# Three split passes instead of full-width products in the 128-row groups of a second MoE (one core)

## The chip, the core and the metric

The kernel runs on one core of a Trainium2 chip. The metric is device time in microseconds, from one launch of the whole chain (attention, first MoE, second MoE). The engines are named as the profile names them: PE (TensorE's matmuls; PEld its weight loads), DVE (VectorE), ACT (ScalarE), POOL (GpSimd) and SP (SyncE, which issues most DMAs).

## What is computed

The reference, cut to the part that the change touches (before it come a windowed attention and a dense MLP with softplus, whose output is `x` here):

```python
def _moe2_ref(x, w_gate, w_noise, noise, w1, w2):      # x 2304 x 512, 8 experts
    ...                                                # noisy logits, top2 and weights top2_w
    for e in range(E):
        for k in range(2):
            mask = top2[:, k] == e
            h = np.maximum(x[mask] @ w1[e], 0.0)       # w1[e] 512 x 1024
            out[mask] += top2_w[mask, k, None] * (h @ w2[e])   # w2[e] 1024 x 512
    return out
```

All of it is float32.

## The kernel before, in words

The kernel writes its own order of instructions: a small planner (`Order`) keeps a clock of its own with a cost for each step, and emits ACT, DVE, POOL and SP work from a heap as PE's matmuls are written out. An engine then runs its instructions in that order. Attention and the first MoE end about 690 us into the run; the rest, what is looked at here, is the second MoE.

**Groups.** The routed rows of each expert are cut into groups of 256 rows ("pairs", `n == 2`) and of 128 rows ("singles", `n == 1`). The list `groups` holds 4 early pairs, 14 later pairs and 5 singles that always run, in the order 4 + 2 pairs, single, 3 pairs, single, 3 pairs, single, 6 pairs, single, single. Two further singles stand behind a condition and do not run with this input. A group gathers its rows from DRAM by an indirect DMA on POOL (`xg`), transposes them on PE (`g_transpose`), multiplies by `w1` (step `s1`, "up"), and by `w2` (step `s3`, "down"), and adds the weighted result to the output by an indirect DMA on POOL. A pair has 8 up and 8 down steps of 128 hidden columns; a single has 2 up and 2 down steps of 512, with a transpose of the relu output between them (`s2`), since it computes rows by hidden columns and not hidden columns by rows.

**The order on PE.** `phase2(x)` issues `s1` of step x, then a transpose for the next group if one is due, then `s2` of step x-1; the loop then issues `s3` of step x-2. The steps of all groups stand in one list, so around a single S the order is: up step 7 of the pair before, down 5; S up 0, transpose for the next group, down 6; S up 1, transpose for the next group, transpose of S's relu output 0, down 7; up 0 of the next group, transpose of S's relu output 1, S down 0; up 1 of the next group, S down 1.

**Precision.** A pair does its float32 products as three passes: each operand is cut into a high part (float32r, made by ACT) and a low part (the rest, made by DVE), and high x high, high x low and low x high are added up in PSUM (`up`, line 524, and `down`, line 536). A single takes its raw float32 weights and its float32 input in one plain product.

**Weights.** A group needs 8 pieces of 128 x 1024, 512 KB each: 4 of `w1` (kind 0) and 4 of `w2` (kind 1). `WJ` lists all pieces in one order, for a pair w1, w2, w1, w2, ..., for a single its 4 of w1 and then its 4 of w2 (line 1076). `w2_load` (line 1088) loads them in this order into 4 extra buffers and into a ring of 24 buffers. `w2_split` (line 1128) takes the next loaded piece, makes `whi` on ACT and `wlo` on DVE in two ring buffers, and gives the raw buffer back (`w2_drop`). At most `NSPLIT = 5` pieces are split and not yet used up. `w2_free` (line 1159) is called when PE has used a piece for the last time: it counts `nsplit` down for a split piece (for a raw one it gives the raw buffer back) and calls `pump`, which loads and splits what now has room. `skip_singles` moves the splitting past the pieces of singles.

The lines of the count, before the change:

```python
        if j >= wl[0] or not splitting[0] or nsplit[0] >= NSPLIT or nback[0] < len(sidx) or ring_left() < 2:
            return False
        wsp[0] += 1
        nsplit[0] += 1
        ...
        chain(("A", ca(1024), lambda: ACT.activation(hi, t, AF.Copy), None, (("r2", j),)),
              ("V", cv(1024), low, ("w2", j)))
```

Of the kernel before, what the change touches and what calls it, by code (L numbers as in the profile page):

```python
# [18 lines left out]
P = 128  # L19
# [6 lines left out]
class Order:  # L26
# [11 lines left out]
    def chain(self, *steps, after=0.0):  # L38

        heapq.heappush(self.heap, (self.now + after, self.count, steps, 0))  # L40
        self.count += 1
# [54 lines left out]
def ca(n):  # L96
    return 0.16 + n * 0.00083


def cv(n):  # L100
    return 0.15 + n * 0.00104
# [11 lines left out]
def moe_chain_kernel(ctx, tc, qk, v, w_in, w_out, w_gate, w_noise, noise, w1, w2, out):  # L113
# [939 lines left out]
    def g_transpose(g, a):  # L1053
        n, eo, i = groups[g]
        d = GR[g]
        pt = ps_t(("gx", g, a)).rearrange("p (c t) -> p c t", c=KC)
        for kc in range(KC):
            tr(pt[:, kc, :], d["xg"][a][:, kc * P:(kc + 1) * P], ident)
        if n == 1:
            d["xT"] = tl(p2, [P, KC, P], F32, "xs", 2, ("gup", g))  # L1060
            return chain(("A", ca(512), lambda: ACT.activation(d["xT"], pt, AF.Copy), ("gx", g, a)))
        if a == 0:
            d["xT"] = tuple(tl(mid, [P, KC, CT], F32R, x, 2, ("gup", g)) for x in ("xh", "xl"))
        xh, xl = d["xT"]
        sl = slice(a * P, (a + 1) * P)
        chain(("A", ca(512), lambda: ACT.activation(xh[:, :, sl], pt, AF.Copy)),
              ("V", cv(512), lambda: DVE.tensor_sub(xl[:, :, sl], pt, f32(xh[:, :, sl])), ("gx", g, a)))
# [20 lines left out]
    def w2_load():  # L1088
        j = wl[0]
        if j >= NW:  # L1090
            return False
        g, kind, f = WJ[j]
        if g >= sure[0] or ("tab", 2 if groups[g][0] == 1 else int(g >= NEARLY)) not in o_.fin:
            return False
        more = len(extra) < NXTRA
        if not more and (nback[0] < len(sidx) or ring_left() < 1 + 2 * max(1, NSPLIT - nsplit[0])):
            return False
        wl[0] += 1
        n, eo, i = groups[g]
        if g not in REG:  # L1100
            REG[g] = SP.value_load(TB[eo][0:1, 0, i:i + 1], min_val=0, max_val=E - 1)
            g_rows(g)
            if g < 3 or g - 3 in turned:
                g_start(g)
        if more:
            extra.add(j)
            t = p2.tile([P, 1024], F32, name="raw2", tag="raw2", bufs=NXTRA)
        else:
            inring[0] += 1
            t = wpool.tile([P, 1024], F32, name="rawp", tag="w", bufs=NRING)  # L1110
        RAW2[j] = t
        SP.dma_start(t, (w2 if kind else w1)[bass.ds(REG[g], 1), f].rearrange("e p n -> p (e n)"))
        chain(("SP", 0.5, None), ("DMA", (1 << 19) / 280e3, None), (None, 2.5, None, ("r2" if n == 2 else "w2", j)))
        if n == 1 and wsp[0] == j:
            skip_singles()
        return True

    turned = set()
# [2 lines left out]
        n = groups[g][0]  # L1121
        chain(("P", 1.3 * n, lambda: g_gather(g), ("gg", g), (("rows", g),)), (None, 3.0, None, ("gl", g)))

    def skip_singles():
        while wsp[0] < wl[0] and groups[WJ[wsp[0]][0]][0] == 1:
            wsp[0] += 1

    def w2_split():
        skip_singles()
        j = wsp[0]  # L1130
        if j >= wl[0] or not splitting[0] or nsplit[0] >= NSPLIT or nback[0] < len(sidx) or ring_left() < 2:
            return False
        wsp[0] += 1
        nsplit[0] += 1
        t = RAW2[j]
        hi, lo = W2[j] = [wpool.tile([P, 1024], F32R, name=x, tag="w", bufs=NRING) for x in ("whi", "wlo")]

        def low():
            DVE.tensor_sub(lo, t, f32(hi))  # L1139
            w2_drop(j)  # L1140
        chain(("A", ca(1024), lambda: ACT.activation(hi, t, AF.Copy), None, (("r2", j),)),  # L1141
              ("V", cv(1024), low, ("w2", j)))
        return True
# [13 lines left out]
                pass  # L1157

    def w2_free(j):
        if W2.pop(j, None) is None:  # L1160
            w2_drop(j)
        else:
            nsplit[0] -= 1
        pump()

    def parts(j, a):
        hl = W2[j]
        if WJ[j][1] == 0:
            return lambda z, kc: hl[z][:, kc * 256 + a * P:kc * 256 + (a + 1) * P]
        return lambda z: hl[z][:, a * 512:(a + 1) * 512]  # L1170
# [4 lines left out]
    def s1(g, f):  # L1175
        n = groups[g][0]
        if n == 2:
            j = WJ.index((g, 0, f // 2))
            need(("w2", j))
            for a in range(2):  # L1180
                need(("gx", g, a))
            ph = up(parts(j, f % 2), GR[g]["xT"], CT, ("hr2", g, f))
            if f % 2:
                w2_free(j)
            gh = tl(mid, [P, CT], F32R, "gh", 4, ("dn", g, f))
            gl = tl(mid, [P, CT], F32R, "gl", 4, ("dn", g, f))
            chain(("A", ca(CT), lambda: ACT.activation(gh, ph, AF.Relu)),
                  ("V", cv(CT), lambda: DVE.scalar_tensor_tensor(gl, ph, 0.0, f32(gh), op0=OP.max, op1=OP.subtract),  # L1188
                   ("hr2", g, f)))
            H2[g, f] = (gh, gl)  # L1190
        else:
            need(("gx", g, 0))
            ph = tl(psum, [P, 512], F32, "h", 2, ("hr2", g, f))
            for x in range(2):
                j = WJ.index((g, 0, 2 * f + x))
                need(("w2", j))
                for kc in range(KC):
                    mm(ph[:, x * 256:(x + 1) * 256], GR[g]["xT"][:, kc, :],
                       RAW2[j][:, kc * 256:(kc + 1) * 256], kc == 0, kc == KC - 1)
                w2_free(j)  # L1200
            hs = tl(p2, [P, 512], F32, "hs", 2, ("ht", g, f))
            chain(("A", ca(512), lambda: ACT.activation(hs, ph, AF.Relu), ("hr2", g, f)))
            H2[g, f] = hs
        if f == (NF1 if n == 2 else 2) - 1:
            mark(("gup", g))

    def s2(g, f):
        if groups[g][0] == 2:
            return
        need(("hr2", g, f))  # L1210
        hs = H2[g, f]
        pt = ps_t(("hT", g, f)).rearrange("p (c t) -> p c t", c=4)
        for x in range(4):
            tr(pt[:, x, :], hs[:, x * P:(x + 1) * P], ident)
        mark(("ht", g, f))
        th = tl(p2, [P, 4, P], F32, "th", 2, ("dn", g, f))
        chain(("A", ca(512), lambda: ACT.activation(th, pt, AF.Copy), ("hT", g, f)))
        H2[g, f] = th

    def s3(g, f):  # L1220
        n = groups[g][0]
        if f == 0:
            yt, tag = ("y", "y") if g % 2 else ("z", "t")
            Y2[g] = [tl(psum, [P, 512], F32, yt, 2, ("ye", g, a), tag, 2 if g % 2 else 4) for a in range(n)]
        if n == 2:
            j = WJ.index((g, 1, f // 2))
            need(("w2", j))
            need(("hr2", g, f))
            gh, gl = H2.pop((g, f))
            down(Y2[g], gh, gl, parts(j, f % 2), f == 0, f == NF1 - 1)  # L1230
            if f % 2:
                w2_free(j)
        else:
            need(("hT", g, f))
            th = H2.pop((g, f))
            for x in range(4):
                ff = 4 * f + x
                j = WJ.index((g, 1, ff // 2))
                need(("w2", j))
                mm(Y2[g][0], th[:, x, :], RAW2[j][:, x % 2 * 512:x % 2 * 512 + 512], ff == 0, ff == NF1 - 1)  # L1240
                if x % 2:
                    w2_free(j)
        mark(("dn", g, f))
        if f == (NF1 if n == 2 else 2) - 1:
            rc = GR[g]["rc"]
            for a in range(n):
                ys = tl(p2, [P, DM], F32, "ys", 4, ("yo", g, a))
                def put(ys=ys, a=a):
                    POOL.indirect_dma_start(  # L1249
                        out=out[:, :], out_offset=bass.IndirectOffsetOnAxis(ap=rc[:, a, 0:1], axis=0),  # L1250
                        in_=ys, in_offset=None, compute_op=OP.add)
                    if a == n - 1:
                        mark(("gdone", g))
                if a == 0:
                    ev = ("A", ca(512) + 0.1, lambda ys=ys: ACT.activation(
                        ys, Y2[g][0], AF.Copy, scale=f32(rc[:, 0, 1:2])), ("ye", g, 0))
                else:
                    ev = ("V", cv(512), lambda ys=ys: DVE.tensor_scalar(  # L1258
                        ys, Y2[g][1], f32(rc[:, 1, 1:2]), None, op0=OP.mult), ("ye", g, 1))
                chain(ev, ("P", 1.1, put, ("yo", g, a)))  # L1260
# [191 lines left out]
```

## Time and profile before

| what | value |
|---|---|
| median of 3 runs | 1137.41 us (1136.45 to 1138.78) |
| the profiled execution | 1136.42 us |
| its span, first to last instruction | 1134.2 us |
| mean granted TensorE clock | 0.978 of 2.4 GHz |
| PE, DVE, ACT busy | 94%, 66%, 54% |

The profile is of one execution. Busy times of PE are of overlapping, pipelined matmuls; the chain of waits gives the time that a run of them takes. In the timeline a row is start, length, engine, line, operation and tiles (out<-in), and in brackets the idle time in front of it with what ended it. The line of all matmuls is that of a helper, so the tiles tell what they are: `h` is the output of an up step, `y` or `z` that of a down step, `t` that of a transpose. `raw` and `rawp` are raw weight pieces, `xs` and `xh`/`xl` inputs of a group, `hs` and `th` relu outputs of a single, `gh`/`gl` those of a pair. A plain float32 product shows as two matmul records.

### The profile page before, as it was taken

How to read it: one execution, taken by the hardware profiler on the slowest of the kernel's cores; microseconds unless marked ns; L12 is line 12 of the kernel's file. 1: busy time of each engine (PE TensorE's matmuls, PEld its weight loads, DVE VectorE, ACT ScalarE, POOL GpSimd, SP SyncE). 2: the span in 40 equal slices, each digit the busy share in tenths (PEclk: the TensorE clock that was granted, in tenths of full speed). 3: DMA queues.
4: the chain of work that ended last, by engine and by line, in shares of the span. 5: the costliest groups of instructions: out<-in, count | busy, mean ns of one | idle time of the engine just before them, and what ended most of it. 6: DMA issues, size and time to landing. Idle time of an engine off the chain costs nothing.

```text
span 1134.2 us, 20933 instructions
## 1 busy us (share of the span) xinstructions
PE 1071.8 (94%) x7021; PEld 914.2 (81%) x7021; DVE 748.8 (66%) x1946; ACT 616.2 (54%) x1459; POOL 509.9 (45%) x535
## 2 busy tenths in 40 slices
PE   5589999999999999999998997999999999999997
PEld 3477777777789888888887886997997997999984
DVE  8975799988885677777767685653653653655520
ACT  7876778877764444444444543553553553555531
POOL 3455677766675566666674232222122223222112
PEclk8699999999999999999999998999999999999999
DMA  8231544554683322112348829788887888888722
GB/s 306 102 94 57 181 161 141 202 206 146 199 318 121 121 76 75 52 62 76 96 153 304 251 28 339 206 233 263 227 233 259 232 227 254 250 225 233 215 56 38
DMA packets 96557, 198.90 MB, mean 175 GB/s; under 512 B 34049, under 2 KB 44801, under 8 KB 96449
## 3 DMA queue, kind: packets, MB, share of 16 engines
q1 hardware_dynamic: 86112, 176.01, 47.2%
q0 software_dynamic: 10336, 21.54, 9.6%
q8 instruction: 56, 0.92, 0.3%
q14 instruction: 53, 0.43, 0.1%
HBM read 157.82 MB, written 39.69 MB: 174 GB/s over the span
## 4 chain that ended last, share of the span: by engine, by line
PE 76%; DVE 11%; DMA 5%; ACT 3%; issue 2%; POOL 1%; SPq 1%; POOLq 0%; DVEq 0%; ACTq 0%
PE h L190 35%; PE y L190 24%; PE z L190 10%; PE t L201 4%; PE t L190 3%; PE t L339 2%; DMA raw<-in_moe_w_out 1%; DVE s L350 1%; ACT s L356 1%; DVE w L504 1%; DVE cva L495 1%; DMA rawp<-in_moe_w 1%; DVE cva L496 1%; DVE cva L494 1%; DVE su L573 1%
## 5 line engine op out<-in xcount | busy, mean ns | idle before, releaser
L190 PE MATMUL h<-xh,w 128*128 128x256 f32 x1152 | 238.8, 290 | 4.3 <-DVE sl L568 4.2
L1139 DVE TENSOR_TENSOR wlo<-rawp,whi 128x1024 fp32r<-128x1024 f32 x107 | 130.7, 1222 | 133.8 <-ACT whi L1141 127.4
L1249 POOL DMA_INDIRECT out<-ys,rc x41 | 83.3, 2031 | 272.3 <-DVE ys L1258 131.9
L190 PEld LDWEIGHTS h<-xh,w 128*128 128x128 f32 x1152 | 190.7, 193 | 18.2 <-DVE sl L568 9.3
L1141 ACT ACTIVATE whi<-rawp 128x1024 fp32r<-128x1024 f32 x107 | 113.4, 1060 | 149.1 <-PE h L190 98.0
L190 PE MATMUL y<-w,gh 128*128 128x512 f32 x552 | 179.3, 406 | 0.1
L190 PE MATMUL h<-xh,whi 128*128 128x256 f32 x576 | 165.5, 287 | 6.5 <-DVE gl L1188 6.5
L190 PE MATMUL h<-xl,w 128*128 128x256 f32 x576 | 164.2, 285 | 3.1 <-DVE xl L434 3.1
L574 POOL TENSOR_TENSOR su<-sa,su 128x256 f32<-128x256 f32 x144 | 112.6, 782 | 113.1 <-DVE su L573 98.3
L190 PE MATMUL h<-xl,whi 128*128 128x256 f32 x576 | 163.3, 284 | 0.0
L190 PE MATMUL h<-xh,wlo 128*128 128x256 f32 x576 | 163.3, 283 | 0.0
L565 ACT ACTIVATE sa<-h 128x256 f32<-128x256 f32 x144 | 54.8, 381 | 157.5 <-PE h L190 116.0
L190 PEld LDWEIGHTS h<-xh,whi 128*128 128x128 f32 x576 | 110.1, 191 | 14.1 <-DVE gl L1188 6.9
L569 POOL TENSOR_TENSOR sl<-sl,su 128x256 f32<-128x256 f32 x144 | 109.7, 762 | 17.3 <-DVE sl L568 5.8
L190 PEld LDWEIGHTS h<-xl,w 128*128 128x128 f32 x576 | 111.1, 193 | 6.4 <-DVE xl L434 3.5
L190 PEld LDWEIGHTS h<-xl,whi 128*128 128x128 f32 x576 | 110.2, 191 | 7.1 <-issue 1.4
L190 PEld LDWEIGHTS h<-xh,wlo 128*128 128x128 f32 x576 | 110.2, 191 | 0.0
L190 PEld LDWEIGHTS y<-w,gh 128*128 128x128 f32 x552 | 95.0, 191 | 16.9 <-issue 3.2
L190 PE MATMUL y<-w,gl 128*128 128x512 f32 x276 | 108.6, 393 | 0.0
L1048 POOL DMA_INDIRECT xg<-x1buf,rc x41 | 42.4, 1035 | 105.6 <-DVE rc L1037 60.4
L572 DVE TENSOR_TENSOR gl<-sl,gh 128x256 fp32r<-128x256 f32 x144 | 81.0, 563 | 9.4 <-ACT gh L570 6.6
L370 POOL TENSOR_TENSOR s<-s,st 128x512 f32<-128x512 f32 (+2 forms) x72 | 72.2, 1011 | 33.2 <-DVE st L362 19.4
(256 smaller groups left out, 2281.5 us busy)
## 6 DMA issues: line engine op xcount, KB each, us to landing
rawp<-in_moe_w SPq DMA_DIRECT2D x140, 512.0 KB
raw<-in_moe_w SPq DMA_DIRECT2D x44, 512.0 KB
qkT<-in_qk SPq DMA_DIRECT2D x20, 512.0 KB
raw<-in_moe_w_in SPq DMA_DIRECT2D x16, 512.0 KB
raw<-in_moe_w_out SPq DMA_DIRECT2D x16, 512.0 KB
out<-zero SPq DMA_DIRECT2D x19, 256.0 KB
xspill<-xh SPq DMA_DIRECT2D x9, 512.0 KB
xspill<-xl SPq DMA_DIRECT2D x9, 512.0 KB
```

Of the source, the lines that this page charges most:

```text
L190: PE.matmul(o, l, r, start=start, stop=stop)
L201: PE.transpose(o, i, idn)
L339: PE.matmul(ps[j][:nq, x, :n].rearrange("p (s t) -> p s t", t=P), qkT[hd, u % NQK, 0, hp, :nq], qkT[hd, sl, 1, hp, :], start=True, stop=True)
L370: POOL.tensor_tensor(s[:nq, :, :n], s[:nq, :, :n], st[:nq, 3, 2 * x:2 * x + 2, None].to_broadcast([nq, 2, n]), OP.mult)
L565: chain(("A", ca(CT), lambda: ACT.activation(a, ph, AF.Abs)), ("A", ca(CT), lambda: ACT.activation(a, a, AF.Exp, scale=-1.0), ("e", t)), ( ...
L569: ("P", cg(CT), lambda: POOL.tensor_add(l, l, u), None, (("d", t),)),
L572: ("V", cv(CT), lambda: DVE.tensor_sub(gl, l, f32(gh)), ("g", t)))
L574: ("P", cg(CT), lambda: POOL.tensor_tensor(u, a, u, OP.subtract), ("d", t)), after=2 * ca(CT) + 0.15)
L1048: POOL.indirect_dma_start(out=x, out_offset=None, in_=x1buf[:T - 3 * CT if g < NEARLY else TPAD, :], in_offset=bass.IndirectOffsetOnAxis(a ...
L1139: DVE.tensor_sub(lo, t, f32(hi))
L1141: chain(("A", ca(1024), lambda: ACT.activation(hi, t, AF.Copy), None, (("r2", j),)), ("V", cv(1024), low, ("w2", j)))
L1249: POOL.indirect_dma_start(out=out[:, :], out_offset=bass.IndirectOffsetOnAxis(ap=rc[:, a, 0:1], axis=0), in_=ys, in_offset=None, compute_o ...
```

## The change

Singles now take split weights, split inputs and split relu outputs, and three passes for each product, as the pairs do. The input of a single goes into the tiles `xh`, `xl` that pairs use; the transposed relu output becomes a high part on ACT and a low part on DVE (`th`, `tl`); the pieces of singles are split in the order of `WJ` like all others, so `skip_singles` goes. `NSPLIT`, the ring, `WJ` and the order on PE stay.

```diff
@@ -1056,9 +1056,6 @@
         pt = ps_t(("gx", g, a)).rearrange("p (c t) -> p c t", c=KC)
         for kc in range(KC):
             tr(pt[:, kc, :], d["xg"][a][:, kc * P:(kc + 1) * P], ident)
-        if n == 1:
-            d["xT"] = tl(p2, [P, KC, P], F32, "xs", 2, ("gup", g))
-            return chain(("A", ca(512), lambda: ACT.activation(d["xT"], pt, AF.Copy), ("gx", g, a)))
         if a == 0:
             d["xT"] = tuple(tl(mid, [P, KC, CT], F32R, x, 2, ("gup", g)) for x in ("xh", "xl"))
         xh, xl = d["xT"]
@@ -1110,9 +1107,7 @@
             t = wpool.tile([P, 1024], F32, name="rawp", tag="w", bufs=NRING)
         RAW2[j] = t
         SP.dma_start(t, (w2 if kind else w1)[bass.ds(REG[g], 1), f].rearrange("e p n -> p (e n)"))
-        chain(("SP", 0.5, None), ("DMA", (1 << 19) / 280e3, None), (None, 2.5, None, ("r2" if n == 2 else "w2", j)))
-        if n == 1 and wsp[0] == j:
-            skip_singles()
+        chain(("SP", 0.5, None), ("DMA", (1 << 19) / 280e3, None), (None, 2.5, None, ("r2", j)))
         return True
 
     turned = set()
@@ -1121,12 +1116,7 @@
         n = groups[g][0]
         chain(("P", 1.3 * n, lambda: g_gather(g), ("gg", g), (("rows", g),)), (None, 3.0, None, ("gl", g)))
 
-    def skip_singles():
-        while wsp[0] < wl[0] and groups[WJ[wsp[0]][0]][0] == 1:
-            wsp[0] += 1
-
     def w2_split():
-        skip_singles()
         j = wsp[0]
         if j >= wl[0] or not splitting[0] or nsplit[0] >= NSPLIT or nback[0] < len(sidx) or ring_left() < 2:
             return False
@@ -1157,14 +1147,14 @@
                 pass
 
     def w2_free(j):
-        if W2.pop(j, None) is None:
-            w2_drop(j)
-        else:
-            nsplit[0] -= 1
+        del W2[j]
+        nsplit[0] -= 1
         pump()
 
-    def parts(j, a):
+    def parts(j, a=None):
         hl = W2[j]
+        if a is None:
+            return lambda z, kc: hl[z][:, kc * 256:(kc + 1) * 256]
         if WJ[j][1] == 0:
             return lambda z, kc: hl[z][:, kc * 256 + a * P:kc * 256 + (a + 1) * P]
         return lambda z: hl[z][:, a * 512:(a + 1) * 512]
@@ -1194,9 +1184,12 @@
             for x in range(2):
                 j = WJ.index((g, 0, 2 * f + x))
                 need(("w2", j))
+                w = parts(j)
+                xh, xl = GR[g]["xT"]
                 for kc in range(KC):
-                    mm(ph[:, x * 256:(x + 1) * 256], GR[g]["xT"][:, kc, :],
-                       RAW2[j][:, kc * 256:(kc + 1) * 256], kc == 0, kc == KC - 1)
+                    for n_, (l, r) in enumerate(((xh, 0), (xh, 1), (xl, 0))):
+                        mm(ph[:, x * 256:(x + 1) * 256], l[:, kc, :P], w(r, kc),
+                           kc + n_ == 0, kc == KC - 1 and n_ == 2)
                 w2_free(j)
             hs = tl(p2, [P, 512], F32, "hs", 2, ("ht", g, f))
             chain(("A", ca(512), lambda: ACT.activation(hs, ph, AF.Relu), ("hr2", g, f)))
@@ -1213,8 +1206,9 @@
         for x in range(4):
             tr(pt[:, x, :], hs[:, x * P:(x + 1) * P], ident)
         mark(("ht", g, f))
-        th = tl(p2, [P, 4, P], F32, "th", 2, ("dn", g, f))
-        chain(("A", ca(512), lambda: ACT.activation(th, pt, AF.Copy), ("hT", g, f)))
+        th = [tl(p2, [P, 4, P], F32R, x, 2, ("dn", g, f)) for x in ("th", "tl")]
+        chain(("A", ca(512), lambda: ACT.activation(th[0], pt, AF.Copy)),
+              ("V", cv(512), lambda: DVE.tensor_sub(th[1], pt, f32(th[0])), ("hT", g, f)))
         H2[g, f] = th
 
     def s3(g, f):
@@ -1237,7 +1231,9 @@
                 ff = 4 * f + x
                 j = WJ.index((g, 1, ff // 2))
                 need(("w2", j))
-                mm(Y2[g][0], th[:, x, :], RAW2[j][:, x % 2 * 512:x % 2 * 512 + 512], ff == 0, ff == NF1 - 1)
+                w = parts(j, x % 2)
+                for n_, (l, r) in enumerate(((0, 0), (0, 1), (1, 0))):
+                    mm(Y2[g][0], th[l][:, x, :], w(r), ff + n_ == 0, ff == NF1 - 1 and n_ == 2)
                 if x % 2:
                     w2_free(j)
         mark(("dn", g, f))
```

## Rows read from the trace of the kernel before

**Rows 1.** The page: span, and busy time, share and instructions of three engines.
```profile
span 1134.2 us, 20933 instructions
...
PE 1071.8 (94%) x7021; PEld 914.2 (81%) x7021; DVE 748.8 (66%) x1946; ACT 616.2 (54%) x1459; POOL 509.9 (45%) x535
```

**Rows 2.** Chain of waits in order of time (start, length, what) around the first single.
```profile
767.87 3.46 PE h L190 x16
...
773.15 3.46 PE h L190 x16
776.61 0.87 PE t L201 x8
777.48 1.39 PE y L190 x6
778.87 1.42 PE h L190 x12
780.29 0.44 PE t L201 x4
780.73 3.44 PE z L190 x8
```

**Rows 3.** Timeline of PE: three rows with idle time in front, 600 to 700 us.
```profile
603.60 0.39 PE L190 MATMUL h<-xh,w 128*128 128x256 f32 x1 [3.27 <-DVE sl L568]
...
652.63 0.18 PE L190 MATMUL t<-mcum,ones 128*128 128x8 bf16 x1 [1.97 <-DVE mcum L757]
...
698.75 0.58 PE L190 MATMUL h<-xh,whi 128*128 128x256 f32 x1 [6.49 <-DVE gl L1188]
```

**Rows 4.** Windows: length, busy PE, PEld, DVE, ACT, POOL, clock, DMA share, GB/s.
```profile
768.00:789.00 21.00, 21.00 (x102) 15.75 (x101) 7.62 (x12) 7.58 (x12) 2.63 (x2) 1.00 0.87 263
...
1094.00:1104.00 10.00, 10.00 (x52) 8.63 (x51) 0.00 (x0) 2.06 (x4) 0.00 (x0) 1.00 0.00 0
```

**Rows 5.** Timeline of ACT between the first single and the next pair.
```profile
776.64 0.60 ACT L1202 ACTIVATE hs<-h 128x512 f32<-128x512 f32 x1 [4.20 <-PE h L190]
777.14 0.59 ACT L1066 ACTIVATE xh<-t 128x512 fp32r<-128x512 f32 x1
777.61 0.61 ACT L1217 ACTIVATE th<-t 128x512 f32<-128x512 f32 x1
778.67 1.06 ACT L1141 ACTIVATE whi<-rawp 128x1024 fp32r<-128x1024 f32 x1 [0.45 <-PE y L190]
779.64 0.67 ACT L1255 ACTIVATE ys<-y,rc 128x512 f32<-128x512 f32 x1
```

**Rows 6.** Timeline of DVE in the same stretch.
```profile
777.76 0.69 DVE L1067 TENSOR_TENSOR xl<-t,xh 128x512 fp32r<-128x512 f32 x1 [4.59 <-ACT xh L1066]
778.91 0.75 DVE L1258 TENSOR_SCALAR ys<-y,rc 128x512 f32<-128x512 f32 x1 [0.46 <-PE y L190]
779.77 1.23 DVE L1139 TENSOR_TENSOR wlo<-rawp,whi 128x1024 fp32r<-128x1024 f32 x1
```

**Rows 7.** Timeline of POOL: the last scatter-adds of the run.
```profile
1105.88 1.55 POOL L1249 DMA_INDIRECT out<-ys,rc  x1 [17.09 <-DVE ys L1258]
1111.24 1.55 POOL L1249 DMA_INDIRECT out<-ys,rc  x1 [3.81 <-DMA out<-ys,rc]
1120.46 1.55 POOL L1249 DMA_INDIRECT out<-ys,rc  x1 [7.67 <-ACT ys L1255]
1127.77 1.55 POOL L1249 DMA_INDIRECT out<-ys,rc  x1 [5.75 <-ACT ys L1255]
```

**Rows 8.** Timeline of DVE: three low parts of weights one after the other.
```profile
596.26 3.49 DVE L1139 TENSOR_TENSOR wlo<-raw,whi 128x1024 fp32r<-128x1024 f32 x3
```

**Rows 9.** Windows of 5 us behind the first two rows of group 3.
```profile
600.00:605.00 5.00, 1.73 (x9) 1.40 (x8) 4.96 (x10) 1.60 (x7) 2.54 (x4) 0.89 0.56 146
605.00:610.00 5.00, 5.00 (x30) 4.77 (x29) 3.70 (x15) 1.71 (x4) 3.16 (x5) 0.77 0.89 335
...
650.00:655.00 5.00, 3.03 (x21) 2.53 (x21) 3.59 (x10) 2.87 (x4) 0.31 (x1) 1.00 0.67 152
655.00:660.00 5.00, 5.00 (x35) 4.53 (x34) 4.55 (x15) 2.69 (x5) 3.76 (x3) 1.00 0.42 55
```

## The prediction, made before the changed kernel ran

> **What bounds the kernel now.** First the page's head: the matrix engine (PE) is busy 1071.8 of 1134.2 us, VectorE (DVE) 66%, ScalarE (ACT) 54% [rows 1]. Then the chain of waits in order of time, around the first group of 128 rows (I call it S; there are five that always run): it is PE alone, piece after piece without a gap [rows 2]. The last idle stretch of PE that another engine ends starts its matmul at 698.75 us [rows 3]; behind it the second MoE is PE-bound, in the windows of S and of the last two groups too, where DVE and ACT are little over a third busy or less [rows 4]. So a microsecond of PE saved in S is a microsecond of the span, as long as nothing new makes PE wait.
>
> **What the change takes off PE.** In S one up step is 8 plain products of 128x256, shown as 16 halves, 3.46 us; one down step is 8 halves of 128x512 for 4 products, 3.44 us [rows 2]. Afterwards the up step is 2 pieces x 4 chunks x 3 = 24 matmuls of the pairs' form, of which 12 take 1.42 us: 2.84. The down step is 4 x 3 = 12 matmuls of 128x512, of which 6 take 1.39: 2.78 [rows 2]. Saved: 0.62 + 0.66 = 1.28 per step, 2.56 per group, 5 groups: **12.8 us**. The Trainium skill (FP8 and Floating Point Precision, TensorE Precision Notes) counts a true FP32 product as four passes, so that three would save a quarter. The rows of the same shapes give 0.62 of 3.46, under a fifth; by the page's rule the five groups would save a quarter of 13.80 each, 17.3 us.
>
> **What it adds off PE.** 8 pieces of S are now split, each one whi on ACT (1.06) and one wlo on DVE (1.23) [rows 5, 6], 40 of each in all; 10 low parts of the relu outputs and 5 of the inputs on DVE, each like xl, 0.69 [rows 6]. Per group that is 8 x 1.23 + 3 x 0.69 = 11.9 us of DVE, in a stretch where DVE has worked 7.6 of 21 us [rows 4]: it fits as a sum. The input's low part is made four pair steps ahead; the low part of a relu output has the next group's up step to hide in, and would cost at most its 0.69 without it. No transfer is added, SP's queue issues the same loads, and its raw buffers come free no later than before, as a split ends before PE's use. All loads are down by 1094 us (DMA share 0.00) [rows 4], so the last splits don't wait for one. The last scatter-adds on POOL stand 7.31 us apart, and 5.36 where one waits for the other's DMA [rows 7]; two down steps less 2 x 0.66 leave 5.99, still over 5.36. What follows PE's last matmul stays.
>
> **The wait that it adds.** At most NSPLIT = 5 pieces may be split and not yet used up (w2_split, w2_free). Until now S's pieces were skipped, so that the five were the next pair's. Now they are taken in WJ's order: S's four w1, its four w2, then the next group's first w1. But PE goes S up 0, S up 1, the last down step of the pair before, **the next group's up step**, and only then S down 0 (phase2 runs s1 two steps ahead of s3). When PE gets to the next group's up step, S's four w2 pieces are still unused; the fifth place is held by the last w2 piece of the pair before, which is given back at the end of the down step that PE has just done. So the split that PE needs now begins now, and PE, which works in order, stands. Today the split that begins at this point (778.67, after the down step at 777.48) is for later use [rows 2, 5].
>
> Its length: the least is whi at once, 1.06, then wlo, 1.23, and the step of 0.04 between an engine's end and the next one's start (779.73 to 779.77 [rows 5, 6]) twice, less the two matmuls that need no wlo (0.24): **2.1 us**. With the queues as they will stand, counted from the end E of S up 1: PE is at the next group after two sets of transposes and a down step, 0.87 + 1.39 = 2.26. ACT, by the steps in [rows 5], does the whi of S's last piece (its place came free at E) to 1.0, hs to 1.5, xh to 2.0, th to 2.5, and only then the wanted whi, to 3.6. DVE does the wlo of that piece from 1.1 (a step of 1.13, by a third of the 3.49 [rows 8], plus its end), xl, the new low part, ys, each 0.6 to 0.7, and reaches the wanted wlo at 4.1; it ends at 5.35, PE goes on at 5.4: 5.4 - 2.26 - 0.24 = **2.9**. One more wlo in front would make it 4.0. I take 2.9, since every piece of the queue has its row, for each of the three groups that stand between pairs; 2.1 and 4.0 stay as ends.
>
> The last two groups follow one another. The first wait is 2.8, by the same queue without xl, and with PE there at 1.83. Then the second w1 piece of the last group gets its place only when the first is used up, within the same up step: queues empty, 1.06 + 1.23 + 0.08, less one matmul of 0.12, **2.3**. Further on every piece has 2.8 us of PE work or more ahead of it, against 2.3.
>
> **Sum.** Waits 3 x 2.9 + 2.8 + 2.3 = 13.8; saved 12.8; net **+1.0 us**. With the least waits, 4 x 2.1 + 2.3 = 10.7, it is -2.1; with 4.0 three times, +4.3. The profiled execution took 1136.42 us (span 1134.2), 0.99 less than the median of the three runs, 1137.41. I put the difference on the median: **1138.4 us**. A measurement of this kernel can tell about 0.2%, 2.3 us, from no change. So the change moves about 13 us of work and should show next to nothing.
>
> **Rivals.**
> - *The clock falls in the new gaps (slower).* After PE's gap of 3.27 us that ended at 603.60 [rows 3] the mean granted clock was 0.89 and 0.77 in the two 5 us windows: (0.11 + 0.23) x 5 = 1.7 us lost; after the gap of 1.97 that ended at 652.63 it stayed 1.00 [rows 9]. The new gaps lie between, at 2.1 to 2.9, with one or two matmuls inside; from somewhere there it falls to 1.2 GHz for a while. Five times would be +8.5, three times, which I take, +5.1 on the sum: 1143.5 us. The Trainium skill (TensorE: Matmul & The Clock Gate, A second HAM failure mode: psum-queue depth-cycling) speaks for it: repeated short idles between groups of matmuls can cost the clock although no single one is long. Of short gaps the trace of before has the one at 652.63, which speaks against. Chance 0.25.
> - *PE does not wait (faster).* If the next group's first piece were split in time, through a place that comes free earlier than I read it, all 12.8 is gain: 1124.6 us. For it: PE has not waited for a split since 698.75 [rows 3], and DVE and ACT have the time [rows 4]. Against it: the order in WJ and the count of five leave no place, whatever the engines' leisure. Chance 0.14.
> - *The waits are there but shorter (faster).* If ACT and DVE come to the wanted split before the rest of their queues, and the last two groups wait once, it is 4 x 2.1 = 8.4 less 12.8: -4.4, 1133.0 us. Against it: instructions of an engine stand in the order of emission. Chance 0.08.
> - *A pass costs a quarter of a plain product.* As a mechanism: 24 up matmuls in three quarters of 3.46, 12 down ones in three quarters of 3.44. That saves 17.3 and nets 13.8 - 17.3 = -3.5: 1133.9 us. The same shapes in the pairs speak against it [rows 2]. Chance 0.03. It is the rule named above from the Trainium skill's page.
>
> **How the numbers follow.** The forecast itself has 0.50; of that 0.06 is for waits towards 4.0, past +2.3, the rest is within 0.2%. Faster: 0.14 + 0.08 + 0.03 = 0.25. Same: 0.44. Slower: 0.25 + 0.06 = 0.31. Range: 1130 to 1145. It takes in the sum with both its ends (1135.3 to 1141.7), the shorter waits, the page's count, and the clock with three falls and nearly four (1138.4 + 6.8 = 1145.2); left out are the case without waits, 0.14, and some 0.05 of the clock's. As faster and slower cases hold half the chance, the likeliest case's own range: 1135 to 1142.
>
> **What would show it.** Right: up steps of S at 2 x 1.43 and down steps at 2.78; PE idle 2 to 3 us behind the down step that follows S up 1, ended by wlo, three times, and twice more ahead of and inside the last group's first up step; 40 more whi and wlo; the first difference in time at S, some 770 us in. The step on the clock is judged by the windows behind each gap: 1.00 or below. Wrong: no PE idle <-DVE wlo at these places (the whole 12.8 shows), or PE waiting at others too, as for a low part of a relu output, a raw load or xl; or the span of a group without its waits not 2.6 us shorter.

## The result: some 0.4% slower, four of the five waits as forecast and the clock on top

The changed kernel took 1143.28 us (median of 5 runs), the kernel before beside it 1136.45; the ratio is 1.0055 (95% interval 1.0040 to 1.0069). In a second set of runs (below) it was 1.0033 (1.0019 to 1.0046). So it is slower by some 0.4%, 4 to 7 us. The forecast was 1138.4 in a range of 1130 to 1145, with "within 0.2%" as the likeliest case; what came is the rival in which the clock falls in the new gaps, at 1143.5. That the two numbers stand 0.2 apart is partly luck: the part of the run that the change touches is 4.6 us longer, where the rival had 6.1, and the rest of this set's difference lies elsewhere (below).

The head of the page after the change, and the low parts of its weights ([rows 1] before):

```profile
span 1142.5 us, 21308 instructions
...
PE 1067.1 (93%) x7141; PEld 924.4 (81%) x7141; DVE 803.8 (70%) x2001; ACT 656.2 (57%) x1499; POOL 507.7 (44%) x535
...
L1129 DVE TENSOR_TENSOR wlo<-rawp,whi 128x1024 fp32r<-128x1024 f32 x140 | 170.5, 1222 | 134.7 <-ACT whi L1131 128.0
```

PE is busy 5 us less and the span is 8 us longer: PE stands more. Of DVE's 55 us more, 49 are the 40 additional `wlo` (1.22 us each). The chain of waits in order of time, around the first single ([rows 2] before; "..." stands for rows left out):

```profile
771.58 2.87 PE h L190 x24
...
776.29 2.86 PE h L190 x24
...
780.02 1.40 PE y L190 x6
...
784.59 2.31 PE h L190 x10
...
787.74 3.08 PE z L190 x12
...
792.27 2.79 PE z L190 x12
```

The up steps take 2.87 (3.46 before), the later down step 2.79 (3.44): the saving is there. But behind the `y` step that ends at 781.42 PE's next row is at 784.59 (between them the chain runs through DVE), and the ten matmuls in it take 2.31 us, which is 0.23 each; where nothing waits twelve take 1.44, 0.12 each (below). PE's timeline at this place, then ACT's and DVE's:

```profile
782.70 0.39 PE L190 MATMUL h<-xh,whi 128*128 128x256 f32 x1 [1.29 <-ACT whi L1131]
782.93 0.31 PE L190 MATMUL h<-xl,whi 128*128 128x256 f32 x1
784.59 0.38 PE L190 MATMUL h<-xh,wlo 128*128 128x256 f32 x1 [1.34 <-DVE wlo L1129]
```

```profile
779.19 1.06 ACT L1131 ACTIVATE whi<-rawp 128x1024 fp32r<-128x1024 f32 x1 [0.50 <-PE h L190]
780.15 0.58 ACT L1195 ACTIVATE hs<-h 128x512 f32<-128x512 f32 x1
780.63 0.59 ACT L1063 ACTIVATE xh<-t 128x512 fp32r<-128x512 f32 x1
781.11 0.60 ACT L1210 ACTIVATE th<-t 128x512 fp32r<-128x512 f32 x1
781.59 1.06 ACT L1131 ACTIVATE whi<-rawp 128x1024 fp32r<-128x1024 f32 x1
```

```profile
780.28 1.23 DVE L1129 TENSOR_TENSOR wlo<-rawp,whi 128x1024 fp32r<-128x1024 f32 x1 [0.34 <-ACT whi L1131]
781.45 0.75 DVE L1254 TENSOR_SCALAR ys<-y,rc 128x512 f32<-128x512 f32 x1
782.12 0.68 DVE L1064 TENSOR_TENSOR xl<-t,xh 128x512 fp32r<-128x512 f32 x1
782.72 0.68 DVE L1211 TENSOR_TENSOR tl<-t,th 128x512 fp32r<-128x512 f32 x1
783.31 1.22 DVE L1129 TENSOR_TENSOR wlo<-rawp,whi 128x1024 fp32r<-128x1024 f32 x1
```

These are the two queues of the forecast: whi, hs, xh, th, whi on ACT; wlo, ys, xl, the low part of the relu output (`tl`) and wlo on DVE, where only `ys` stands first of the three and not last. From 781.42 to 784.59 are 3.17 us, of which two matmuls work 0.24: a wait of 2.93, where 2.9 stood. The same stands at the two other singles between pairs.

At the last two groups it differs. PE is at the last group's first up step at 1112.73, when the down step in front of it ends; first its row in the chain, then PE's timeline and ACT's:

```profile
1111.32 1.41 PE z L190 x6
```

```profile
1113.00 0.38 PE L190 MATMUL h<-whi,xh 128*128 128x256 f32 x1 [0.29 <-ACT whi L1131]
...
1115.29 0.38 PE L190 MATMUL h<-wlo,xh 128*128 128x256 f32 x1 [1.90 <-DVE wlo L1129]
```

```profile
1111.89 1.06 ACT L1131 ACTIVATE whi<-rawp 128x1024 fp32r<-128x1024 f32 x1
...
1113.41 2.01 ACT L1131 ACTIVATE whi<-rawp 128x1024 fp32r<-128x1024 f32 x2
```

One wait, with one matmul inside it, and no second one: the whi of the second piece starts at 1113.41, when PE has hardly begun with the first. Counted as above, from 1112.73 to 1115.29 less one matmul of 0.12, it is 2.4 us.

Now the clock behind the four waits, in windows of 4 us ([rows 9] before have the columns of such rows):

```profile
784.00:788.00 4.00, 3.42 (x16) 3.32 (x17) 0.95 (x2) 0.60 (x2) 0.10 (x1) 0.61 1.02 291
788.00:792.00 4.00, 4.00 (x24) 3.51 (x23) 2.10 (x5) 2.50 (x3) 3.31 (x3) 0.97 0.55 82
...
872.00:876.00 4.00, 3.73 (x18) 3.44 (x19) 1.39 (x5) 0.98 (x2) 0.00 (x0) 0.70 1.05 292
876.00:880.00 4.00, 4.00 (x22) 3.45 (x21) 1.65 (x4) 2.12 (x3) 2.34 (x2) 0.87 0.34 75
...
960.00:964.00 4.00, 4.00 (x24) 3.57 (x25) 1.26 (x4) 1.95 (x3) 0.55 (x1) 1.00 0.86 224
...
1116.00:1120.00 4.00, 4.00 (x25) 4.00 (x23) 1.50 (x2) 0.12 (x1) 0.57 (x1) 0.58 0.42 59
```

Behind the first wait the clock lost (0.39 + 0.03) x 4 = 1.7 us, behind the second (0.30 + 0.13) x 4 = 1.7, behind the third nothing, behind the fourth 0.42 x 4 = 1.7. Three of four, 5.1 us; behind the first, from 785 to 788 us, the granted clock was 0.50 of 2.4 GHz, the lower of its two levels (1.2 GHz).

**One measure for all runs.** The stages ahead of the second MoE vary from execution to execution: the same row of the attention stage starts at 111.65 us in this profile and at 108.76 in the second profile of the same kernel.

```profile
111.65 1.10 PE L339 MATMUL t<-qkT 64*128 64x256 f32 x6 [0.54 <-DVE sdl L434]
```

```profile
108.76 1.10 PE L339 MATMUL t<-qkT 64*128 64x256 f32 x6 [0.53 <-DVE sdl L434]
```

So I compare the **stretch** from the start of the first single's first up step to the issue of the last scatter-add on POOL. Before it is 1127.77 - 767.87 = 359.90 us [rows 2, 7]; after the change 1136.10 - 771.58 = 364.52, that is +4.62.

```profile
1136.10 1.55 POOL L1245 DMA_INDIRECT out<-ys,rc  x1 [4.46 <-ACT ys L1251]
```

In the table the stretch is that of one profiled execution; the ratio is that of all runs to the kernel before, run beside them.

| kernel | first single at | stretch, us | against before | ratio of the runs (95%) |
|---|---|---|---|---|
| before | 767.87 | 359.90 | | |
| changed | 771.58 | 364.52 | +4.62 | 1.0055 (1.0040 to 1.0069) |
| changed, second set | 767.46 | 364.60 | +4.70 | 1.0033 (1.0019 to 1.0046) |
| six places | 763.47 | 353.56 | -6.34 | 0.9902 (0.9880 to 0.9924) |
| seven places | 760.64 | 352.30 | -7.60 | 0.9877 (0.9853 to 0.9901) |
| order of use | 767.77 | 352.29 | -7.61 | 0.9945 (0.9924 to 0.9966) |
| up step only | 772.37 | 358.80 | -1.10 | 0.9988 (0.9974 to 1.0002) |
| gaps filled | 768.79 | 359.81 | -0.09 | 1.0003 (0.9988 to 1.0017) |
| before, seven places | 763.81 | 359.90 | 0.00 | 0.9929 (0.9911 to 0.9948) |
| all together | 762.66 | 347.55 | -12.35 | 0.9837 (0.9816 to 0.9858) |
| order and transposes | 769.20 | 347.54 | -12.36 | 0.9907 (0.9891 to 0.9923) |

### The profile page after: what moved, and what is told of

Same layout as the page of the kernel before. It is cut to its first block, busy times and chain, and to the rows that moved or that the text cites. A ratio compares the mean times of both kernels' runs of the same rounds, so it can differ in the third digit from the quotient of the medians.

```text
span 1142.5 us, 21308 instructions
## 1 busy us (share of the span) xinstructions
PE 1067.1 (93%) x7141; PEld 924.4 (81%) x7141; DVE 803.8 (70%) x2001; ACT 656.2 (57%) x1499; POOL 507.7 (44%) x535
## 4 chain that ended last, share of the span: by engine, by line
PE 78%; DVE 12%; DMA 4%; ACT 3%; issue 2%; SPq 1%; POOL 1%; POOLq 0%; DVEq 0%; ACTq 0%
PE h L190 35%; PE y L190 24%; PE z L190 9%; PE t L201 4%; PE t L190 3%; PE t L339 2%; DVE s L350 2%; ACT s L356 1%; DVE cva L495 1%; DVE cva L496 1%; DVE wlo L1129 1%; DVE cva L494 1%; DVE gl L572 1%; DVE w L504 1%; DMA rk<-rect 1%
## 5 line engine op out<-in xcount | busy, mean ns | idle before, releaser
L1129 DVE TENSOR_TENSOR wlo<-rawp,whi 128x1024 fp32r<-128x1024 f32 x140 | 170.5, 1222 | 134.7 <-ACT whi L1131 128.0
L1131 ACT ACTIVATE whi<-rawp 128x1024 fp32r<-128x1024 f32 x140 | 148.0, 1061 | 153.3 <-PE h L190 99.5
L1245 POOL DMA_INDIRECT out<-ys,rc x41 | 80.9, 1973 | 259.7 <-DVE ys L1254 126.0
L573 DVE TENSOR_SCALAR su<-sa 128x256 f32<-128x256 f32 x144 | 60.1, 418 | 39.9 <-ACT sa L566 36.1
```

Source lines behind the costliest of these rows:

```text
L573: chain(("V", cv2(CT), lambda: DVE.tensor_scalar(u, a, 1.0, 1.0, op0=OP.add, op1=OP.subtract), None, (("e", t),)), ("P", cg(CT), lambda: P ...
L1245: POOL.indirect_dma_start(out=out[:, :], out_offset=bass.IndirectOffsetOnAxis(ap=rc[:, a, 0:1], axis=0), in_=ys, in_offset=None, compute_o ...
```

## The experiments

Each changes the changed kernel, but for one that runs it once more and one that changes the kernel before. Theory A is that the next group's first piece gets its place among the five too late; B, that ACT and DVE can't keep up; C, that the late first single in the first profile belongs to the changed program.

**More places.** `NSPLIT = 5` becomes 6, then 7.

> The changed kernel with six pieces allowed to be split ahead instead of five. Theory A (the next group's first piece gets its place only when PE already wants it): with a sixth place its split begins at the end of the single's second up step, 2.3 us before PE wants it. The whi wait goes; what is left is a wait of about 0.6 us for the low part of the next pair's input. No gap is over 2 us, so the clock stays at 1.00. Against the changed kernel (1143.3): 3 x 2.3 + 1.8 less waiting and about 5 us less lost to the clock, some 1130 us. Theory B (ACT and DVE can't split 8 pieces in the time of a single): the waits stay at 2.5 to 3 us, 1143 us. Theory C (the 3.7 us by which the profiled execution was late already before the first single belong to the changed program): they show here too, before 770 us.

> Seven places. Theory A: the split begins in the middle of the second up step, 3.7 us ahead; no wait for weights at the five places, so about the whole 12.8 us saved against the kernel before, 1124 to 1127 us. Theory B: 1143 us, waits as with five. Theory C: 3 to 4 us more than A says, with the lateness before the first single.

Measured 1127.21 us and 1123.53, the kernel before beside them 1139.80. The waits for weights went, but for one of 1.0 us with six places at the last group. B falls. In their place PE waits three times, 1.3 us at the longest, for the low part of the next pair's input: about the 0.6 us that I had put there for six places, doubled, and one that I had not put there at all for seven. The clock stays at 1.00 behind these. And both kernels have the first single 4 us and more earlier than the kernel before, which A does not explain; see the seven places by themselves below. So it is luck that 1123.53 stands next to A's 1124 to 1127: by the stretches the changed kernel with seven places is 7.6 us shorter than the kernel before, not 12.8.

**The order of use.**

```diff
             WJ += [(g, kind, f) for kind in range(2) for f in range(NW1)]
+    for g in range(sure[0] - 1):
+        if groups[g][0] == 1:
+            for f, at in ((0, 0), (1, 0), (2, 2), (3, 2))[:1 if groups[g + 1][0] == 2 else 4]:
+                WJ.remove((g + 1, 0, f))
+                WJ.insert(WJ.index((g, 1, at)), (g + 1, 0, f))
```

> Five places as in the changed kernel, but the list of pieces puts the next group's first w1 piece ahead of a single's four w2 pieces (and, between the last two singles, all of the pieces in the order of their use). Theory A: the waits at the next group's up step go, as with seven places: 1124 to 1127 us. Theory B: the same splitting work in the same time, waits of 2.5 to 3 us stay somewhere around each single: 1140 to 1143 us. Theory C: 3 to 4 us more than A says.

1132.44 us. No wait for weights, with five places and the same splitting work: this is the place in the list, not the engines' leisure. The time is 5 to 8 us over what A said. Of that 4.75 us are a wait that stood hidden behind the other (by the stretches, against the last run below, in which it is gone); the rest is not accounted for, but the kernel before beside it, at 1139.80, was 2.4 over the 1137.41 that A's figure started from.

```profile
779.05 0.39 PE L190 MATMUL h<-xl,whi 128*128 128x256 f32 x1 [1.20 <-DVE xl L1064]
```

```profile
776.47 1.23 DVE L1134 TENSOR_TENSOR wlo<-rawp,whi 128x1024 fp32r<-128x1024 f32 x1 [0.34 <-ACT whi L1136]
777.64 0.75 DVE L1259 TENSOR_SCALAR ys<-y,rc 128x512 f32<-128x512 f32 x1
778.31 0.68 DVE L1064 TENSOR_TENSOR xl<-t,xh 128x512 fp32r<-128x512 f32 x1
```

The low part of the next pair's input stands behind a wlo and a ys on DVE. In the kernel before it had DVE to itself at this point [rows 6].

**The up step alone.** `w2` pieces and relu outputs of singles stay plain:

```diff
-        th = [tl(p2, [P, 4, P], F32R, x, 2, ("dn", g, f)) for x in ("th", "tl")]
+        th = tl(p2, [P, 4, P], F32, "th", 2, ("dn", g, f))
...
-                for n_, (l, r) in enumerate(((0, 0), (0, 1), (1, 0))):
-                    mm(Y2[g][0], th[l][:, x, :], w(r), ff + n_ == 0, ff == NF1 - 1 and n_ == 2)
+                mm(Y2[g][0], th[:, x, :], RAW2[j][:, x % 2 * 512:x % 2 * 512 + 512], ff == 0, ff == NF1 - 1)
```

> Only the up step of singles takes three passes; their w2 pieces and relu outputs stay plain float32 as in the kernel before. Theory A: w2 pieces hold no place, so the next group's piece is split early: no wait. Saved are two up steps of 0.6 us in five groups, 6.1 us against the kernel before, 1130.4 us. Theory B: half the splitting work, so about half the waits, and no clear gain: 1133 to 1137 us.

1137.64 us against 1139.80: no difference that can be told from none. The weights' wait is gone, as A says, but the time is nearer to B's. The stretch says why: of the 5.9 us saved (ten up steps at 2.87 for 3.46), three waits of 1.2 for the same xl, which cost 1.6 each as in the order of use, leave -1.10.

**The gaps filled.** 24 matmuls of the group's input with itself before the next pair's first up step, 20 before the last group's; the real product then overwrites them.

```diff
+    def fill(o, x, n, k):
+        for i in range(k):
+            PE.matmul(o[:, :n], x[:, i % KC, :P], x[:, i % KC, :n], start=True, stop=True)
...
+        if gap:
+            fill(ph, xh, n, 24)
...
+                if g == sure[0] - 1 and f == x == 0:
+                    fill(ph, xh, P, 20)
```

> The changed kernel, with matmuls that nobody needs put on PE where it waited: 24 of 128x256 before the next pair's first up step (three places), 20 of 128x128 before the last group's, written to the same PSUM tile and overwritten by the real ones. About 2.8 us of PE work each time, so the splits end as they did, but PE is not idle. If the idle gaps made the clock fall (theory A, second part): the granted clock stays at 1.00 after all four places, the stretch from the first single's first up step to the last scatter-add takes 364.5 - 5.1 = 359.4 us, and the run some 5 us less than the changed kernel. If the clock falls for another cause, or the loss isn't the clock's: 364 us or more.

1138.39 us, 3.5 less than the unaltered kernel beside it (1141.89); the stretch is 359.81, where 359.4 was expected. The fillers take the place of the waits (0.2 us of waiting is left at the last group), and the clock behind them stays up:

```profile
778.62 3.00 PE h L526 x24
...
864.70 2.99 PE h L526 x24
...
950.78 3.00 PE h L526 x24
```

```profile
782.00:786.00 4.00, 4.00 (x25) 3.56 (x25) 1.29 (x5) 2.05 (x3) 0.76 (x1) 1.00 0.82 214
...
868.00:872.00 4.00, 4.00 (x25) 3.56 (x26) 1.26 (x4) 2.03 (x3) 0.00 (x0) 1.00 1.02 277
...
954.00:958.00 4.00, 4.00 (x25) 3.57 (x25) 1.27 (x4) 1.95 (x3) 0.00 (x0) 1.00 0.91 240
...
1110.00:1114.00 4.00, 4.00 (x31) 3.74 (x30) 2.00 (x3) 1.62 (x3) 0.71 (x1) 1.00 0.44 63
```

So the 5 us are the clock's (4.7 and 4.8 by the stretches of the two profiles of the changed kernel), and idleness of PE is its cause. The single groups say the same: from a single's first up step to the third up step of the pair behind it are 21.9 us with the gap filled, 21.9 where the unfilled gap kept the clock, and 23.5 where it lost it, in both profiles of the changed kernel.

**The changed kernel again.**

> The changed kernel once more, unaltered. If it is chance which of the four gaps costs the clock: between two and four of them do, 1.7 us each, and the stretch from the first single on takes 362.8 to 366.2 us. If the 3.7 us by which its profile was late before the first single belong to the program (theory C), the first single starts at 771 to 772 us again; if they are chance, somewhere between 766 and 772.

1141.89 us, the kernel before beside it 1137.88. The stretch is 364.60. Again three of the four gaps cost the clock, but not the same three:

```profile
780.00:784.00 4.00, 3.54 (x17) 3.35 (x18) 1.09 (x3) 0.98 (x2) 0.16 (x1) 0.67 0.97 276
...
871.00:875.00 4.00, 4.00 (x25) 3.51 (x24) 2.82 (x5) 2.85 (x3) 1.90 (x1) 1.00 0.69 227
...
957.00:961.00 4.00, 4.00 (x18) 3.27 (x17) 1.98 (x4) 1.76 (x3) 0.48 (x1) 0.76 0.26 86
...
1114.00:1118.00 4.00, 4.00 (x20) 3.65 (x20) 0.94 (x2) 2.43 (x4) 1.55 (x1) 0.76 0.22 20
```

The first single starts at 767.46 this time: C falls, the lateness was chance. The two profiled executions took 1144.45 and 1140.32 us, and the whole difference of 4.1 lies ahead of the first single, as the stretches agree within 0.1 us. That the two ratios differ for the same reason is likely, but not shown.

**Seven places in the kernel before.** `NSPLIT = 7` there.

> The kernel before, with seven places instead of five. Its singles hold no place, so theory A expects nothing of it from the first single on: 359.9 us as before. What six and seven places gained ahead of the first single (no wait of 6 us for the pair's low part of the relu output near 698 us) should show here alone: 5 to 7 us less than the kernel before.

1131.74 us against 1137.88, 6.1 less; the stretch is that of before to the hundredth. PE's wait of 6.49 us that ended at 698.75 [rows 3] is gone. So this gain has nothing to do with singles, and the runs with six and seven places must be read by the stretch. Why that wait goes with more places stays open.

**All together, and without the places.** The order of use, and both transposes for the next pair behind a single's first up step; with seven places and with five.

```diff
-            if g + 1 < sure[0] and f in ((last - 4, last - 2) if last > 1 else (0, 1)):
+            if g + 1 < sure[0] and f in ((last - 4, last - 2) if last > 1 else (0,)):
...
+                if last == 1 and groups[g + 1][0] == 2:
+                    a = 1
+                    g_transpose(g + 1, a)
```

> The changed kernel with pieces in the order of use, seven places, and both transposes for the next pair right after a single's first up step (the three waits of 1.2 us for the low part of the next pair's input, which six and seven places and the order of use left). From the first single on 352.3 - 3 x 1.5 = 348 us; with the 5 to 7 us ahead of it some 17 to 19 us less than the kernel before. If those waits were ACT's and DVE's queues and not the late transpose, 352 us stay.

> Five places, pieces in the order of use, both transposes for the next pair right after a single's first up step: the last run but without the seven places. If its stretch from the first single on was short because of these two, it is 347.6 us again here, 12.3 less than the kernel before, and the start of the first single (counted from the end of the attention stage) is as in the kernel before, 659 us: some 1.1% less in all. If the places had a part in it, 349 us or more.

1120.06 us (ratio 0.9837) and 1125.57 (0.9907); the stretches are 347.55 and 347.54, so the places had no part in it. In the run with five places the first single comes 659.25 us after the row of the attention stage, in the kernel before 659.11; that row is not the end of this stage, as the expectation has it (its last `t<-qkT` in the kernel before starts at 291.6 us). PE waits for nothing behind the first single's start. The chain of the second of the two:

```profile
769.20 2.87 PE h L190 x24
772.07 0.87 PE t L201 x8
772.94 1.39 PE y L190 x6
774.33 2.88 PE h L190 x24
777.21 0.44 PE t L201 x4
777.65 1.39 PE y L190 x6
779.04 1.44 PE h L190 x12
780.48 0.44 PE t L201 x4
780.91 2.81 PE z L190 x12
```

Here the twelve matmuls of the next pair's up step follow the `y` step at once, in 1.44 us. This is what the three passes are worth when nothing waits for them: 12.36 us.

## Why the prediction held in its range and missed in its likeliest case

- **What PE saves: right.** 12.8 us were worked out from rows of the same shapes, 12.36 came. The rival of a quarter per pass, 17.3, is refuted for this kernel: the plain products are 3.44 to 3.46 a step and the three passes 2.79 to 2.88.
- **What ACT, DVE and the transfers add: right, as a sum.** No wait for raw weights or for a relu output's low part appeared. B is refuted by the order of use.
- **The wait between singles and pairs: right.** The step that named the fifth place, and the queues on both engines, came as written, but for the place of `ys`: 2.93 for 2.9. Against the kernel where nothing waits, a gap that did not cost the clock (the third single's) takes 3.2 us, since the first matmuls behind a wait stand 0.2 apart and not 0.12 (782.70 and 782.93 above). The other two take 4.75 each, of which 1.7 are the clock's.
- **The waits at the last two groups: one of two.** The first was 2.5 us by the stretches (2.8 said). The second, 2.3 us, was not there. The step that failed took "a place comes free when PE has used the piece" for a wait of the engine. The count of five only sets where a split stands in the list of instructions: the second whi at 1113.41 stands right behind `ys` on ACT and waits for nothing. By the code the split itself needs only a free ring buffer; that some are free towards the end because no loads are left to come is argued, not shown.
- **The clock: the step that missed.** The forecast kept it at 1.00, as the gap of 1.97 us had left it there and the one of 3.27 had not [rows 3, 9], and gave a fall 0.25. Gaps of 1.3 + 1.3 us with two matmuls between, or 0.3 + 1.9 with one, cost it in three cases of four, in both profiles, and with the gaps filled it stayed. The price per fall (1.7 us) and the number of falls put into the rival (three) were both met; the price had its rows, the three had none and is luck. In the second set the median, 1141.89, lies just inside the likeliest case's own range of 1135 to 1142, with the same falls: there the number was met and the mechanism missed.

The sum as it came, for the stretch: -12.4 saved, + 3.2 + 2 x 3.05 + 2.5 = 11.8 for the waits, + 5.1 for the clock, together +4.5; measured +4.62. Without the clock's 5.1 it would have been -0.6 (by the stretches the clock took 4.7 to 4.8), and the kernel with the gaps filled has -0.09: by the waits alone the change moves nothing, as forecast.

## What to carry to other kernels

A limit on work prepared ahead must count in the order in which the work is used; where one kind of work begins to take part in such a limit, walk through the places at the seam, piece by piece. When a gap on PE is priced, add the clock behind it to the wait itself: here a wait of 3 us cost 4.8 in three cases of four. A wait that is removed may have hidden the next one on the same engine, so look at what stands behind it in the queue.

## What had not been expected of the hardware

Which gaps cost the clock changed between two executions with the same waits (the third single's in one, the second's in the other was spared). Gaps of 1.2 to 1.3 us alone left it at 1.00 in the windows behind all twelve between singles and pairs (three each with six places, seven places, the order of use and the up step alone). A single gap of 3.0 us does not decide it either: with more places PE waits that long for `mcum` some 655 us in, where the kernel before waits 1.97 [rows 3]. Behind it the two windows of 4 us have 0.63 and 0.95 with six places, 0.66 and 0.92 with seven places in the kernel before, 0.65 and 0.93 with all together, about 1.7 us lost each time, but 1.00 and 1.00 with seven places in the changed kernel. What decides in between stays open.
